# One core, attention over a cached context with a feed-forward beside it: softmax maxima and head blocks moved from TensorE to VectorE, softmax sums taken once at the end, projections in 512 columns

## The chip, the core and the metric

The kernel runs on one core of a Trainium2 chip. The metric is the device time of one execution in microseconds (us), the median of several executions of the same program. Engines are named as the profile names them: PE is TensorE (PEld its weight loads), DVE VectorE, ACT ScalarE, POOL GpSimd, and SP the engine that issues most DMA transfers.

## What is computed

One decoding step for 4 sequences: a layer norm of `x` (4 x 512), then multi-head attention with one query per sequence over a cached context, and beside it a feed-forward layer; both are added to `x`.

```python
xn = _layernorm(x)                                   # (4, 1, 512)
q  = (xn @ wq).reshape(B, 1, 32, 128).transpose(0, 2, 1, 3)
scores = einsum("bhqd,bhkd->bhqk", q, k_cache) * 128 ** -0.5
o  = einsum("bhqk,bhkd->bhqd", softmax(scores), v_cache)
a  = o.transpose(0, 2, 1, 3).reshape(B, 1, 32 * 128) @ wo
f  = silu(xn @ w1) @ w2                              # F = 1792
return x + a + f
```

All data are 32-bit floats. `k_cache` and `v_cache` have shape 4 x 32 x 4096 x 128, 268 MB each; `wq` and `wo` are 8.4 MB each, `w1` and `w2` 3.7 MB each. All of it is read once.

## The kernel before, in words

**Tiles.** The work goes in T = 32 tiles. Tile `i` is one sequence (`b = i % 4`) and a group of G = 4 heads (`h = i // 4 * 4`): 4 x 4096 cached rows, spread as 128 partitions x R = 128 rows x 128 elements (8.4 MB of keys, and as much of values). Partitions 0 to 31 hold head `h`, 32 to 63 head `h + 1`, and so on (PH = 32 partitions a head).

**Buffers and loads.** `load_tile` (L72) issues one transfer on SP's queue. Key tiles have two buffers (`kpool`), value tiles one (`vpool`). In the loop (L328) iteration `i` issues key tile `i + 1` (L330) and value tile `i` (L337), in that order, all on SP, which waits in order: a key load until `sums` of the tile two back has read its buffer, a value load until `values` of the tile before has read the only value buffer. `w1` and `x` lie at first in a key buffer (`scratch`), `wq` in the value buffer; `wo` takes the value buffer at the end and `w2` a key buffer (L352 to L359, `wo` in two pieces, `w2` in four). The last value tile goes into a key buffer (L339).

**Start (L93 to L223).** Constants, layer norm, `xn` transposed; the hidden layer on PE in four strips of columns (L179), SiLU on ACT (L185), 56 small transposing matmuls (L191) into `hT`; the queries in 128 matmuls of 128 columns (L206), regrouped by head (L218) into `q_h`.

**Each tile.** `queries(n)` (L227) copies the queries of a group of four heads over the partitions by four matmuls into a PSUM buffer `q_ps` (two buffers, one per group; a group serves four tiles). `products` (L241) multiplies 32 rows of the key tile by the query on DVE and lets POOL add the two halves of each row; `sums` (L258) reduces each row to its score. `maxima` (L265) reduces a partition's scores on DVE and transposes the 128 maxima on PE (L269). `softmax` (L272) reduces them to one per head on DVE (L275), copies these to all partitions by a matmul (L279) and a scaled copy on ACT (L281), then takes four exponentials on ACT (L285), which also leave each partition's sum in `l`. `values` (L291) does 32 matmuls of 512 columns into one PSUM bank, four groups of 32 output partitions in turn: each row of that bank has a product for each of NR = 4 rows, of which one is wanted. `heads_out` (L305) sums `l` over a head's partitions by a matmul with `same` (L309), copies the bank to SBUF on ACT (L311), and with DVE's reciprocal (L315) and scaled selection matrix `w_t` (L316) adds the wanted blocks into `o_all` by four matmuls of 128 columns (L320).

**Order.** The loop issues `products(i, 0)`, `softmax(i - 1)`, `values(i - 1)`, the rest of the products and sums, `maxima(i)`, `heads_out(i - 1)`, and in every fourth iteration (`i % B == 1`) the queries of the next group. Each engine runs its own stream in order; the framework's scheduler may move an instruction ahead of earlier ones in the program where data and buffers allow it by its own estimate.

**End (L361 to L385).** The last softmax, values and heads; `o_all` copied (L367), transposed by four matmuls (L370) and copied (L375) to `ot`; then `accumulate` (L135) adds each of 32 rows of `wo` and 14 rows of `w2` to `acc` as four matmuls of 128 columns (L138), 184 in all; one copy (L382) and four small output transfers.

Of the kernel before, what the change touches and what calls it, by code (L numbers as in the profile page):

```python
# [8 lines left out]
F32 = mybir.dt.float32  # L9
# [14 lines left out]
def kernel(  # L24
# [29 lines left out]
    FC = F // P  # L54
    PH = P // G
# [27 lines left out]
    FJ = F // 4  # L83
    h_sb = scratch[:, 4 * D : 4 * D + FJ]
# [10 lines left out]
    same = const.tile([P, P], F32, name="same")  # L95
    nc.gpsimd.memset(same, 0.0)
    for g in range(G):
        nc.gpsimd.memset(
            same[g * PH : (g + 1) * PH, :].rearrange("p (a g) -> p a g", g=G)[:, :, g], 1.0
        )  # L100
    one = const.tile([1, 1], F32, name="one")
    nc.gpsimd.memset(one, 1.0)
# [3 lines left out]

    W0 = H - G
    w_t = const.tile([P, NR, W0 + H], F32, name="w_t")
# [15 lines left out]
        o_all.rearrange("h b d -> h (b d)"), w_t[:, 0, :H], p_t.rearrange("p r g -> p (r g)"),  # L124
# [7 lines left out]
        axis=AX, op=ALU.add,  # L132
    )
# [41 lines left out]

    hp = ps_s.tile([P, FJ], F32, name="sm")
    for c in range(DC):
        for j in range(4):
            nc.tensor.matmul(  # L179
                hp[32 * j : 32 * j + B, :], xnT[:, c, :], w1_t[:, c, j * FJ : (j + 1) * FJ],  # L180
                start=(c == 0), stop=(c == DC - 1),
            )
    for j in range(4):
        rows = slice(32 * j, 32 * j + B)
        nc.scalar.activation(h_sb[rows, :], hp[rows, :], AF.Silu)  # L185
    ht_ps = ps_s.tile([P, FC, B], F32, name="sm")
    h_f = h_sb.rearrange("b (m f) -> b f m", f=FC)
    for f in range(FC):
        for j in range(4):
            rows = slice(32 * j, 32 * j + B)  # L190
            nc.tensor.matmul(  # L191
                ht_ps[32 * j : 32 * j + 32, f, :], h_f[rows, f, :], ident[rows, rows],
                start=True, stop=True,
            )
    hT = const.tile([P, FC, B], F32, name="hT")
    nc.vector.tensor_copy(hT, ht_ps)


    HJ = H // 4
    qp = ps_s.tile([P, Dh], F32, name="sm")  # L200
    for hl in range(HJ):
        for c in range(DC):
            for j in range(4):
                h = HJ * j + hl
                a = PH - B - B * hl
                nc.tensor.matmul(  # L206
                    qp[32 * j : 32 * j + 32, :],
                    xpad[:, c, a : a + PH],
                    wq_t[:, c, h * Dh : (h + 1) * Dh],
                    start=(hl == 0 and c == 0),  # L210
                    stop=(hl == HJ - 1 and c == DC - 1),
                )

    q_all = const.tile([P, Dh], F32, name="q_all")
    nc.vector.tensor_copy(q_all, qp)  # L215
    qh_ps = ps_q.tile([P, B, Dh], F32, name="q_ps")
    for b in range(B):
        nc.tensor.matmul(  # L218
            qh_ps[:H, b, :], ident.rearrange("p (h b) -> p b h", b=B)[:, b, :], q_all,
            start=True, stop=True,  # L220
        )
    q_h = const.tile([H, B, Dh], F32, name="q_h")
    nc.vector.tensor_copy(q_h, qh_ps[:H])  # L223

    q_ps, vs, st, ls = {}, {}, {}, {}

    def queries(n):  # L227

        t = ps_q.tile([P, B, Dh], F32, name="q_ps")
        for g in range(G):  # L230
            h = n * G + g
            nc.tensor.matmul(  # L232
                t[g * PH : (g + 1) * PH].rearrange("p b d -> p (b d)"),
                ident[:H, h : h + 1].to_broadcast([H, PH]),
                q_h.rearrange("h b d -> h (b d)"),
# [29 lines left out]
    def maxima(i):  # L265
        m = small.tile([P, 1], F32, name="m")
        nc.vector.tensor_reduce(m, st[i], axis=AX, op=ALU.max)  # L267
        mt = ps_s.tile([1, P], F32, name="sm")
        nc.tensor.transpose(mt, m, ident)  # L269
        return mt  # L270

    def softmax(i, mt):  # L272
        s = st.pop(i)
        gm = small.tile([1, G], F32, name="gm", bufs=1)
        nc.vector.tensor_reduce(  # L275
            gm, mt.rearrange("o (g m) -> o g m", g=G), axis=AX, op=ALU.max
        )
        mb = ps_s.tile([P, G], F32, name="sm")
        nc.tensor.matmul(mb, one.to_broadcast([1, P]), gm, start=True, stop=True)  # L279
        nb = small.tile([P, G], F32, name="nb", bufs=1)  # L280
        nc.scalar.activation(nb, mb, AF.Copy, scale=-scale)  # L281
        l = small.tile([P, 1], F32, name="l_t")
        for g in range(G):
            rows = slice(g * PH, (g + 1) * PH)
            nc.scalar.activation(  # L285
                p_t[rows, :, g], s[rows, :], AF.Exp, bias=nb[rows, g : g + 1], scale=scale,
                accum_out=l[rows, :],
            )
        ls[i] = l

    def values(i):  # L291
        v, o = vs.pop(i), o_ps
        n = R // NR
        for m in range(n):
            j = 32 * (m % 4)
            rows = slice(m * NR, (m + 1) * NR)
            nc.tensor.matmul(  # L297
# [5 lines left out]
            )  # L303

    def heads_out(i):  # L305

        h, b = i // B * G, i % B
        lt = ps_s.tile([P, 1], F32, name="sm")
        nc.tensor.matmul(lt, same, ls.pop(i), start=True, stop=True)  # L309
# [4 lines left out]
        rl = small.tile([P, 1], F32, name="rl", bufs=1)  # L314
        nc.vector.reciprocal(rl, lt)  # L315
        nc.vector.tensor_scalar_mul(  # L316
            w_t[:, :, W0 : W0 + G], pick.rearrange("p (r g) -> p r g", r=NR), rl
        )
        for r in range(NR):
            nc.tensor.matmul(  # L320
                o_all[:, b, :], w_t[:, r, W0 - h : W0 - h + H], o_sb[:, r, :],
# [96 lines left out]
```

## Time and profile before

| | us |
|---|---|
| median of 3 runs | 1310.15 (1309.88 to 1310.94) |
| the profiled execution | 1309.97 |
| its span, first to last instruction | 1307.9 |
| mean granted TensorE clock in it | 0.646 of full speed |

A row of an instruction group reads: line, engine, operation, output and input names, shapes, count, then busy time and mean duration of one in ns, then the idle time of the engine just before and what ended it. A row of the timeline begins with its start and its duration in us; in brackets is the idle time of the engine before it, and what ended that. One 32-bit matmul shows as two matmul records and two weight-load records. A row of a table by stretches has the stretch and its length, then the busy time and count of PE, PEld, DVE, ACT and POOL, then the granted clock, the DMA engines' mean busy share and GB/s. A row of a DMA queue has its packets, MB, and share of 16 engines' span.

### The profile page before, as it was taken

The page shows a single profiled execution, that of the slowest core. Times are in us where ns is not written, and L with a number is a line of the kernel's source. Part 1 is how long each engine was busy: PE and PEld are TensorE (multiplying, and loading weights), DVE is VectorE, ACT ScalarE, POOL GpSimd, SP SyncE. Part 2 cuts the span into 40 slices and gives each one's busy share as a digit, 9 for nine tenths or more (in the row PEclk, how much of TensorE's full clock was granted, in tenths as well). Part 3 has the DMA queues.
Part 4 walks back from the last instruction along what each step waited for, and adds up shares of the span by engine and source line. Part 5 has one row for each costly group of instructions (what it writes and reads, how often), then busy time and mean ns, then how long its engine had stood idle before and what let it go on. Part 6 is the DMA issues. An engine that isn't in the chain of part 4 may idle for free.

```text
span 1307.9 us, 7983 instructions
## 1 busy us (share of the span) xinstructions
PE 397.9 (30%) x3326; PEld 139.1 (11%) x3326; DVE 911.7 (70%) x439; ACT 97.7 (7%) x329; POOL 511.0 (39%) x144
## 2 busy tenths in 40 slices
PE   3412233320333322133332123332043333113337
PEld 1300011100011100011110001110011111001113
DVE  1499666887666787666687666678666678766660
ACT  1010000000000000000000000000000000000000
POOL 0255333444332444332444433344433344433340
PEclk9656666655666656666665666665566665566669
DMA  9999999999999999999999999999999999999997
GB/s 406 440 425 440 427 437 430 435 435 431 438 427 439 429 436 427 435 433 433 434 429 435 429 437 423 439 429 435 429 423 443 422 443 423 443 421 443 425 427 334
DMA packets 10443, 561.51 MB, mean 429 GB/s; under 512 B 1172, under 2 KB 1188, under 8 KB 1448
## 3 DMA queue, kind: packets, MB, share of 16 engines
q1 hardware_dynamic: 10392, 561.01, 99.4%
q8 instruction: 26, 0.43, 0.1%
q14 instruction: 9, 0.07, 0.0%
q10 hardware_dynamic: 16, 0.00, 0.0%
HBM read 561.00 MB, written 0.01 MB: 429 GB/s over the span
## 4 chain that ended last, share of the span: by engine, by line
DMA 66%; PE 17%; DVE 14%; POOL 3%; issue 0%; SPq 0%; POOLq 0%; DVEq 0%
DMA v_t<-in_A_v_cache_dram 34%; DMA k_t<-in_A_k_cache_dram 29%; PE o_ps L297 15%; DVE k_t L247 9%; DVE s L263 4%; DMA k_t<-in_B_w_dram 3%; POOL k_t L251 3%; PE q_ps L232 1%; DVE s L262 0%; PE sm L269 0%; SPq L359 0%; PE acc L138 0%; DVE gm L275 0%; DVE m L267 0%; SPq L87 0%
## 5 line engine op out<-in xcount | busy, mean ns | idle before, releaser
L251 POOL TENSOR_TENSOR k_t<-k_t 128x2048 f32<-128x2048 f32 (+1 forms) x128 | 508.4, 3983 | 749.5 <-DVE k_t L247 749.5
L247 DVE TENSOR_TENSOR k_t<-k_t,q_ps 128x4096 f32<-128x4096 f32 x128 | 562.4, 4414 | 247.8 <-DMA k_t<-in_A_k_cache_dram 247.8
L297 PE MATMUL o_ps<-v_t,p_t 128*16 128x512 f32 x1984 | 283.2, 735 | 628.7 <-DMA v_t<-in_A_v_cache_dram 624.9
L263 DVE TENSOR_REDUCE s<-k_t 128x32 f32<-128x2048 f32 (+1 forms) x128 | 257.7, 2013 | 11.2 <-POOL k_t L251 11.2
L297 PEld LDWEIGHTS o_ps<-v_t,p_t 128*16 128x16 f32 x1984 | 65.4, 113 | 834.6 <-issue 830.8
L311 ACT ACTIVATE o_sb<-o_ps 128x512 f32<-128x512 f32 x32 | 19.1, 597 | 1081.2 <-PE o_ps L297 1081.2
L262 DVE TENSOR_REDUCE s<-k_t 128x16 f32<-128x2048 f32 x32 | 72.8, 2276 | 0.0
L232 PE MATMUL q_ps<-q_h,ident 32*32 32x512 f32 x64 | 14.0, 974 | 183.2 <-DVE k_t L247 182.5
L285 ACT ACTIVATE p_t<-s,nb 32x128 f32<-32x128 f32 x128 | 66.0, 516 | 2.7 <-ACT nb L281 0.2
L275 DVE TENSOR_REDUCE gm<-sm 1x4 f32<-1x128 f32 x32 | 8.9, 278 | 53.7 <-PE sm L269 53.7
L320 PE MATMUL o_all<-o_sb,w_t 128*32 128x128 f32 x256 | 34.0, 276 | 2.4 <-ACT o_sb L311 0.7
L320 PEld LDWEIGHTS o_all<-o_sb,w_t 128*32 128x32 f32 x256 | 25.8, 110 | 5.4 <-ACT o_sb L311 1.6
L285 ACT ACTIVATION_READ_ACCUMULATOR p_t<-s,nb 32x1 f32 x128 | 25.0, 196 | 0.0
L269 PE MATMUL sm<-ident,m 128*1 128x128 f32 x32 | 8.8, 276 | 42.4 <-DVE m L267 41.9
L232 PEld LDWEIGHTS q_ps<-q_h,ident 32*32 32x32 f32 x64 | 1.6, 128 | 185.7 <-DVE k_t L247 184.1
L279 PE MATMUL sm<-gm,one 1*128 1x4 f32 x64 | 12.5, 264 | 11.9 <-DVE gm L275 11.7
L375 DVE COPY ot<-sm 128x128 f32<-128x128 f32 x1 | 0.3, 292 | 19.3 <-PE sm L370 19.3
L215 DVE COPY q_all<-sm 128x128 f32<-128x128 f32 x1 | 0.3, 292 | 17.6 <-PE sm L206 17.6
L206 PE MATMUL sm<-v_t,xpad 128*32 128x128 f32 x256 | 9.8, 327 | 7.9 <-DMA v_t<-in_A_wq_dram 6.0
L281 ACT ACTIVATE nb<-sm 128x4 f32<-128x4 f32 x32 | 5.6, 174 | 84.7 <-PE sm L279 84.7
L297 PE MATMUL o_ps<-k_t,p_t 128*16 128x512 f32 x64 | 9.4, 753 | 6.6 <-DMA k_t<-in_A_v_cache_dram 6.6
L382 DVE COPY s<-acc 128x128 f32<-128x128 f32 x1 | 0.3, 292 | 15.9 <-PE acc L138 15.9
(66 smaller groups left out, 119.0 us busy)
## 6 DMA issues: line engine op xcount, KB each, us to landing
v_t<-in_A_wo_dram SPq DMA_DIRECT2D x2, 4096.0 KB
k_t<-in_B_w_dram SPq DMA_DIRECT2D x1, 3584.0 KB, 11.5
k_t<-in_B_w_dram SPq DMA_DIRECT2D x1, 1792.0 KB, 33.2
k_t<-in_B_w_dram SPq DMA_DIRECT2D x1, 1024.0 KB, 35.9
k_t<-in_A_k_cache_dram SPq DMA_DIRECT2D x32, 48.3
k_t<-in_B_w_dram SPq DMA_DIRECT2D x1, 512.0 KB, 36.7
v_t<-in_A_v_cache_dram SPq DMA_DIRECT2D x31, 29.4
k_t<-in_B_w_dram SPq DMA_DIRECT2D x1, 256.0 KB, 36.9
```

The costliest lines, as they stand in the source:

```text
L206: nc.tensor.matmul(qp[32 * j : 32 * j + 32, :], xpad[:, c, a : a + PH], wq_t[:, c, h * Dh : (h + 1) * Dh], start=(hl == 0 and c == 0), sto ...
L232: nc.tensor.matmul(t[g * PH : (g + 1) * PH].rearrange("p b d -> p (b d)"), ident[:H, h : h + 1].to_broadcast([H, PH]), q_h.rearrange("h b ...
L247: nc.vector.tensor_tensor(k[:, a:z, :], k[:, a:z, :], q[:, None, :].to_broadcast([P, STEP, Dh]), op=ALU.mult)
L251: nc.gpsimd.tensor_tensor(k[:, a:v, :half], k[:, a:v, :half], k[:, a:v, half:], op=ALU.add)
L262: nc.vector.tensor_reduce(s[:, v:z], k[:, v:z, :], axis=AX, op=ALU.add)
L263: nc.vector.tensor_reduce(s[:, a:v], k[:, a:v, :half], axis=AX, op=ALU.add)
L275: nc.vector.tensor_reduce(gm, mt.rearrange("o (g m) -> o g m", g=G), axis=AX, op=ALU.max)
L279: nc.tensor.matmul(mb, one.to_broadcast([1, P]), gm, start=True, stop=True)
L285: nc.scalar.activation(p_t[rows, :, g], s[rows, :], AF.Exp, bias=nb[rows, g : g + 1], scale=scale, accum_out=l[rows, :],)
L297: nc.tensor.matmul(o[j : j + NR * G, :], p_t[:, rows, :].rearrange("p r g -> p (r g)"), v[:, rows, :].rearrange("p r d -> p (r d)"), start ...
L311: nc.scalar.activation(o_sb.rearrange("p r d -> p (r d)"), o_ps, AF.Copy)
L320: nc.tensor.matmul(o_all[:, b, :], w_t[:, r, W0 - h : W0 - h + H], o_sb[:, r, :], start=False, stop=(i == T - 1 and r == NR - 1),)
```

## The change

Per tile: `maxima` stays on DVE. It puts a partition's maximum into column 0 of a zeroed tile of 32 columns, transposes each 32 x 32 block, reduces along the row, scales over 32 columns and transposes back, so that each partition has its head's scaled maximum; the matmuls at L269 and L279, the reduction at L275 and ACT's copy at L281 go. `softmax` leaves its sums in one tile `l_t` for all tiles, and the per-tile matmul (L309), reciprocal and scaling go; the sums are added and inverted once at the end. `heads_out` multiplies the copied bank by a mask `own` and adds the four blocks on DVE, so that one matmul of 128 columns with a fixed selection matrix is left of four.

Order: the first products of a tile are put behind the last instruction of the tile before's `maxima` on DVE (`issue_after(done)`), and the queries of the next group behind the last matmul of `values(i - 1)` in the iterations with `i % B == 2`.

Start and end: the hidden layer is computed in 16 matmuls of up to 512 columns, with the columns of `w1` taken 14 apart, and transposed by four matmuls of 128 columns of a zeroed tile; `wq` in 32 matmuls of 512 columns, with 16 small ones to regroup; `wo` and the first seven rows of `w2` go as 39 matmuls of 512 columns into a bank of their own (`part`, in a `q_ps` buffer), four groups of output partitions in turn, whose copy is added into `acc` by four matmuls; the last seven rows of `w2` are added as before.

```diff
-    h_sb = scratch[:, 4 * D : 4 * D + FJ]
+    h_sb = scratch[:, 4 * D : 4 * D + FT * P]
...
-    same = const.tile([P, P], F32, name="same")
...
+    ones = const.tile([P, 1], F32, name="ones")
+    nc.gpsimd.memset(ones, 1.0)
+    nc.gpsimd.memset(h_sb, 0.0)
...
+    l_t = const.tile([P, B, H // G, G], F32, name="l_t")
+    nc.gpsimd.memset(l_t, 0.0)
+    m_t = const.tile([P, PH], F32, name="m_t")
+    nc.gpsimd.memset(m_t, 0.0)
...
+    nc.vector.tensor_reduce(
+        w_t[:, W0 : W0 + G], pick.rearrange("p (r g) -> p g r", r=NR), axis=AX, op=ALU.add
+    )
+    own = const.tile([P, NR], F32, name="own")
+    nc.vector.tensor_reduce(
+        own, pick.rearrange("p (r g) -> p r g", r=NR), axis=AX, op=ALU.add
     )
...
+    w1_f = w1_t.rearrange("p c (m f) -> p c f m", f=FC)
     for c in range(DC):
         for j in range(4):
             nc.tensor.matmul(
-                hp[32 * j : 32 * j + B, :], xnT[:, c, :], w1_t[:, c, j * FJ : (j + 1) * FJ],
+                hp[32 * j : 32 * j + B, : FN[j] * P],
+                xnT[:, c, :],
+                w1_f[:, c, F0[j] : F0[j] + FN[j], :],
                 start=(c == 0), stop=(c == DC - 1),
             )
...
+    for t in range(FT):
+        nc.tensor.matmul(
+            ht_ps[:, t],
+            h_sb[:, t * P : (t + 1) * P],
+            ident.rearrange("p (j m) -> p j m", j=4)[:, :, :B],
+            start=True, stop=True,
+        )
...
-                    wq_t[:, c, h * Dh : (h + 1) * Dh],
-                    start=(hl == 0 and c == 0),
-                    stop=(hl == HJ - 1 and c == DC - 1),
+                    wq_t[:, c, n * G * Dh : (n + 1) * G * Dh],
+                    start=(m == 0 and c == 0),
+                    stop=(m == NM - 1 and c == DC - 1),
...
     def maxima(i):
-        m = small.tile([P, 1], F32, name="m")
-        nc.vector.tensor_reduce(m, st[i], axis=AX, op=ALU.max)
-        mt = ps_s.tile([1, P], F32, name="sm")
-        nc.tensor.transpose(mt, m, ident)
-        return mt
+        nc.vector.tensor_reduce(m_t[:, :1], st[i], axis=AX, op=ALU.max)
+        mt = small.tile([P, PH], F32, name="mt", bufs=1)
+        nc.vector.transpose(mt, m_t)
+        gm = small.tile([P, 1], F32, name="gm", bufs=1)
+        nc.vector.tensor_reduce(gm, mt, axis=AX, op=ALU.max)
+        mb = small.tile([P, PH], F32, name="mb", bufs=1)
+        nc.vector.tensor_scalar_mul(mb, gm.to_broadcast([P, PH]), -scale)
+        nb = small.tile([P, PH], F32, name="nb", bufs=1)
+        return nb, nc.vector.transpose(nb, mb).ins
 
-    def softmax(i, mt):
+    def softmax(i, nb):
         s = st.pop(i)
...
-        mb = ps_s.tile([P, G], F32, name="sm")
-        nc.tensor.matmul(mb, one.to_broadcast([1, P]), gm, start=True, stop=True)
-        nb = small.tile([P, G], F32, name="nb", bufs=1)
-        nc.scalar.activation(nb, mb, AF.Copy, scale=-scale)
-        l = small.tile([P, 1], F32, name="l_t")
...
-                p_t[rows, :, g], s[rows, :], AF.Exp, bias=nb[rows, g : g + 1], scale=scale,
-                accum_out=l[rows, :],
-            )
-        ls[i] = l
+                p_t[rows, :, g], s[rows, :], AF.Exp, bias=nb[rows, :1], scale=scale,
+                accum_out=l_t[rows, i % B, i // B, g : g + 1],
+            )
...
     def heads_out(i):
-        lt = ps_s.tile([P, 1], F32, name="sm")
-        nc.tensor.matmul(lt, same, ls.pop(i), start=True, stop=True)
...
-        rl = small.tile([P, 1], F32, name="rl", bufs=1)
-        nc.vector.reciprocal(rl, lt)
-        nc.vector.tensor_scalar_mul(
-            w_t[:, :, W0 : W0 + G], pick.rearrange("p (r g) -> p r g", r=NR), rl
-        )
-        for r in range(NR):
-            nc.tensor.matmul(
-                o_all[:, b, :], w_t[:, r, W0 - h : W0 - h + H], o_sb[:, r, :],
-                start=False, stop=(i == T - 1 and r == NR - 1),
-            )
+        nc.vector.tensor_tensor(
+            o_sb, o_sb, own[:, :, None].to_broadcast([P, NR, Dh]), op=ALU.mult
+        )
+        o_1 = small.tile([P, Dh], F32, name="o_1", bufs=1)
+        nc.vector.tensor_reduce(o_1, o_sb.rearrange("p r d -> p d r"), axis=AX, op=ALU.add)
+        nc.tensor.matmul(
+            o_all[:, b, :], w_t[:, W0 - h : W0 - h + H], o_1, start=False, stop=(i == T - 1)
+        )
...
-        products(i, 0)
+        with tc.issue_after(done) if i > 0 else nullcontext():
+            products(i, 0)
         if i > 0:
-            softmax(i - 1, mt)
+            softmax(i - 1, nb)
         if i > 0:
-            values(i - 1)
+            with tc.issue_after(values(i - 1)):
+                if i % B == 2 and i + B < T + 2:
+                    queries(i // B + 1)
...
-        mt = maxima(i)
+        nb, done = maxima(i)
         if i > 0:
             heads_out(i - 1)
-        if i % B == 1 and i + B < T:
-            queries(i // B + 1)
...
+    ls_ps = ps_s.tile([H, B], F32, name="sm")
+    for b in range(B):
+        nc.tensor.matmul(
+            ls_ps[:, b : b + 1], l_t[:, b].rearrange("p n g -> p (n g)"), ones,
+            start=True, stop=True,
+        )
+    rl = const.tile([H, B], F32, name="rl")
+    nc.vector.reciprocal(rl, ls_ps)
     o_row = const.tile([H, B, Dh], F32, name="o_row")
-    nc.scalar.activation(o_row, o_all, AF.Copy)
+    nc.vector.tensor_tensor(
+        o_row, o_all, rl[:, :, None].to_broadcast([H, B, Dh]), op=ALU.mult
+    )
...
-    for c in range(H):
-        accumulate(ot[:, c, :], wo_t[:, c, :])
-    for f in range(FC):
-        accumulate(hT[:, f, :], w2_t[:, f, :], stop=(f == FC - 1))
+    part = ps_q.tile([P, D], F32, name="q_ps")
+    nc.vector.memset(part, 0.0)
+    rows = [(ot[:, c, :], wo_t[:, c, :]) for c in range(H)]
+    rows += [(hT[f], w2_t[:, f, :]) for f in range(W2_CUTS[0])]
+    for c, (a, w) in enumerate(rows):
+        j = 32 * (c % 4)
+        nc.tensor.matmul(
+            part[j : j + B, :], a, w, start=(c < 4), stop=(c >= len(rows) - 4)
+        )
+    part_sb = small.tile([P, NR * Dh], F32, name="o_sb", bufs=1)
+    nc.scalar.activation(part_sb, part, AF.Copy)
+    accumulate(pick[:, :B], part_sb)
+    for f in range(W2_CUTS[0], FC):
+        accumulate(hT[f], w2_t[:, f, :], stop=(f == FC - 1))
```

86 lines of the change are left out of this document (38 added, 48 removed).

## The prediction

> **What bounds the kernel now.** First the page: the engines' busy shares, the DMA queues, the chain that ended last.
>
> ```profile
> PE 397.9 (30%) x3326; PEld 139.1 (11%) x3326; DVE 911.7 (70%) x439; ACT 97.7 (7%) x329; POOL 511.0 (39%) x144
> q1 hardware_dynamic: 10392, 561.01, 99.4%
> q8 instruction: 26, 0.43, 0.1%
> DMA 66%; PE 17%; DVE 14%; POOL 3%; issue 0%; SPq 0%; POOLq 0%; DVEq 0%
> ```
>
> No engine is near its span, but the packets of the data queue fill 99.4% of 16 DMA engines' time. Yet the chain gives PE 17% and DVE 14%. The timeline of one late period tells which is true: SP's issues, the values' start on PE, the next products' start on DVE.
>
> ```profile
> 1188.64 0.33 SPq L76 DMA_DIRECT2D v_t<-in_A_v_cache_dram  x1
> 1189.06 0.38 SPq L76 DMA_DIRECT2D k_t<-in_A_k_cache_dram  x1
> 1197.88 8.75 DVE L247 TENSOR_TENSOR k_t<-k_t,q_ps 128x4096 f32<-128x4096 f32 x2 [8.44 <-DMA k_t<-in_A_k_cache_dram]
> 1217.34 9.37 PE L297 MATMUL o_ps<-v_t,p_t 128*16 128x512 f32 x64 [26.73 <-DMA v_t<-in_A_v_cache_dram]
> 1226.78 0.33 SPq L76 DMA_DIRECT2D v_t<-in_A_v_cache_dram  x1
> 1236.59 8.75 DVE L247 TENSOR_TENSOR k_t<-k_t,q_ps 128x4096 f32<-128x4096 f32 x2 [9.02 <-DMA k_t<-in_A_k_cache_dram]
> ```
>
> The value tile issued at 1188.64 lands near 1217.2, the key tile behind it at 1236.5: one 8.4 MB tile each 19.4 us, one behind the other. PE's 9.37 us do set when the next value load is issued (1226.78), but a key tile is then still in the queue for 9.8 us more. So PE is on the chain of issues and not on that of bytes: the queue has work when the new transfer joins it. All 16 engines together, over the whole middle:
>
> ```profile
> 51.80:1236.60 1184.80, 340.19 (x2361) 107.68 (x2361) 876.08 (x402) 88.75 (x310) 492.54 (x124) 0.63 1.00 433
> 51.80 8.75 DVE L247 TENSOR_TENSOR k_t<-k_t,q_ps 128x4096 f32<-128x4096 f32 x2 [5.25 <-DMA k_t<-in_A_k_cache_dram]
> 148.82 8.75 DVE L247 TENSOR_TENSOR k_t<-k_t,q_ps 128x4096 f32<-128x4096 f32 x2 [9.55 <-DMA k_t<-in_A_k_cache_dram]
> 188.07 8.75 DVE L247 TENSOR_TENSOR k_t<-k_t,q_ps 128x4096 f32<-128x4096 f32 x2 [4.91 <-DMA k_t<-in_A_k_cache_dram]
> ```
>
> The share is 1.00 at 433 GB/s. The key landings show the only loss there: most pairs of tiles take 38.71 us (1197.88 to 1236.59), a few 39.25 (148.82 to 188.07). From 51.80 to 1236.59 there land 31 key and 30 value tiles; at 38.71/2 each that is 1180.7 us, and it took 1184.8: **4.1 us of excess**. What shares the 16 engines is instruction code. PE's 3326 matmul and 3326 weight-load records are 6652 instructions; 0.43 MB over them is 65 bytes each, and 26 packets are 16.5 KB or 256 instructions each. So queue 8 is PE's own program. 0.1% of 16 x 1307.9 us over 26 packets is 0.8 us a packet (0.4 to 1.2 with the rounding), on one engine; a tile has landed when its last engine is done, so the engine hit most often sets the landings. That the excess is these packets is my inference; nothing in the views names it.
>
> **The end**, by the same timeline (value tile 31 lands, then wo in two halves, then w2 in four pieces):
>
> ```profile
> 1275.33 9.39 PE L297 MATMUL o_ps<-k_t,p_t 128*16 128x512 f32 x64 [6.63 <-DMA k_t<-in_A_v_cache_dram]
> 1277.02 0.17 PEld L297 LDWEIGHTS o_ps<-k_t,p_t 128*16 128x16 f32 x4 [0.68 <-issue]
> 1277.87 0.17 PEld L297 LDWEIGHTS o_ps<-k_t,p_t 128*16 128x16 f32 x4 [0.68 <-issue]
> 1282.84 0.11 PEld L297 LDWEIGHTS o_ps<-k_t,p_t 128*16 128x16 f32 x4 [0.32 <-issue]
> 1283.27 0.11 PEld L297 LDWEIGHTS o_ps<-k_t,p_t 128*16 128x16 f32 x4 [0.32 <-issue]
> 1284.80 0.60 ACT L311 ACTIVATE o_sb<-o_ps 128x512 f32<-128x512 f32 x1 [16.54 <-PE o_ps L297]
> 1287.28 1.12 PE L370 MATMUL sm<-o_row,up 32*128 32x128 f32 x8 [0.77 <-ACT o_row L367]
> 1288.44 0.29 DVE L375 COPY ot<-sm 128x128 f32<-128x128 f32 x1 [19.27 <-PE sm L370]
> 1288.79 3.68 PE L138 MATMUL acc<-v_t,ot 128*4 128x128 f32 x128 [0.38 <-DVE ot L375]
> 1294.77 3.68 PE L138 MATMUL acc<-v_t,ot 128*4 128x128 f32 x128 [2.31 <-DMA v_t<-in_A_wo_dram]
> 1299.08 1.06 PE L138 MATMUL acc<-k_t,hT 128*4 128x128 f32 x32 [0.63 <-DMA k_t<-in_B_w_dram]
> 1302.21 1.06 PE L138 MATMUL acc<-k_t,hT 128*4 128x128 f32 x32 [0.20 <-DMA k_t<-in_B_w_dram]
> 1303.49 1.05 PE L138 MATMUL acc<-k_t,hT 128*4 128x128 f32 x24 [0.23 <-DMA k_t<-in_B_w_dram]
> 1304.68 0.29 DVE L382 COPY s<-acc 128x128 f32<-128x128 f32 x1 [15.94 <-PE acc L138]
> ```
>
> PE waits for data at 1294.77, 1299.08, 1302.21 and 1303.49. Only the matmuls behind the very last piece, the copy at 1304.68 and the output lie behind the bytes, and the change leaves these as they are.
>
> **The change, part by part.** *Per tile.* The groups by line and shape give what goes and the prices of what comes:
>
> ```profile
> L320 PE MATMUL o_all<-o_sb,w_t 128*32 128x128 f32 x256 | 34.0, 276 | 2.4 <-ACT o_sb L311 0.7
> L279 PE MATMUL sm<-gm,one 1*128 1x4 f32 x64 | 12.5, 264 | 11.9 <-DVE gm L275 11.7
> L309 PE MATMUL sm<-l_t,same 128*128 128x1 f32 x64 | 9.2, 213 | 1.4 <-ACT p_t L285 1.4
> L267 DVE TENSOR_REDUCE m<-s 128x1 f32<-128x128 f32 x32 | 9.2, 286 | 1.1
> L151 DVE TENSOR_TENSOR k_t<-k_t 4x512 f32<-4x512 f32 x1 | 0.7, 680 | 0.0
> L179 PE MATMUL sm<-k_t,xnT 128*4 128x448 f32 x32 | 4.5, 724 | 0.3 <-DVE xnT L171 0.3
> ```
>
> PE loses 11 of its 77 records a tile (one at L269, two each at L279 and L309, six of eight at L320). DVE gains a multiply and a reduction over 512 elements (0.68 us each) and, in the maxima, two transposes, a reduction and a scaling of 32 columns for two small operations and a reduction that go. Neither that reduction nor a transpose is in the trace; for the first I take L151's time, which has as many elements, for a transpose between nothing and that 0.68 I take L267's 0.29, the nearest by shape. Net some 1.4 + 0.6 = 2 us, at most 3.5. Cover: DVE idles 8 to 10 us for each key tile (the brackets above), and key loads are queued a whole value tile early (1189.06, behind a value load that itself finds the queue full). Price at the end: 0. The new order, first products behind the maxima, costs up to 1.2 us of the same idle time; softmax then starts at once and has 19 us until its value tile lands. If that cover were gone, DVE would have to be late by 8 us.
>
> *Queries behind the values.* In some periods PE now waits for a query buffer with the values queued behind it:
>
> ```profile
> 948.23 1.93 PE L232 MATMUL q_ps<-q_h,ident 32*32 32x512 f32 x8 [30.44 <-DVE k_t L247]
> 960.04 0.33 SPq L76 DMA_DIRECT2D v_t<-in_A_v_cache_dram  x1
> 964.65 8.75 DVE L247 TENSOR_TENSOR k_t<-k_t,q_ps 128x4096 f32<-128x4096 f32 x2 [3.83 <-DMA k_t<-in_A_k_cache_dram]
> ```
>
> The value load is then issued 4.6 us before the key tile in flight lands, not 9.8: late, but not too late. The new place gives the 5 us back; behind the values the buffer is two blocks old, so PE waits for nothing. Price: 0.
>
> *Start.* wq becomes 32 matmuls of 512 columns, as many as one tile's values (9.4 us by the row at 1275.33), and the hidden layer 16 with columns taken 14 apart, which no row shows; between nothing and four times L179's 4.5 us the start's work ends some us earlier to 14 later. Key tile 0 lands at 51.8 whatever they do, and DVE's own work (876 us over 32 tiles, 27 each) then sets the next key load, with a value tile still in the queue. Price: 0.
>
> *End.* From 1284.7: copy 0.6, multiply and reduction 1.4, the head matmul and the sums 0.8, reciprocal and multiply 0.8, transposition 1.1, copy 0.3, some 0.5 of handing over: `ot` at 1290.2 instead of 1288.7. Two matmuls of 512 columns take 0.43 us at full clock (1282.84 to 1283.27), so a half of wo takes 3.4: 1293.6, before 1294.7. The second half ends at 1298.2, before 1299.0; seven rows of w2 take 1.5 to 1300.6. Then PE waits for ScalarE's copy of `part` (0.7) with the last w2 rows queued behind: four small matmuls more, 1301.8, and the next rows come at 1302.1. Slack 1.1, 0.8 and 0.3 us. Price 0, at most +0.5.
>
> *Code.* Matmul records: 352 fewer in the tiles, 192 at L206, 104 at L191, 226 in the projections; 24 more at L218, 8 for the sums: 842 of 3326, **25%**, or 6 to 7 packets of queue 8. A quarter of the 4.1 us of excess is 1.0 us. Bounds: 0, if the same engine is hit as often, and 2.2, if it loses most of its hits.
>
> **Sum:** -1.0 from the profiled execution's 1309.97 us (span 1307.9 and 2.1 around it) is 1309.0; that execution lay 0.2 below the median of the runs, so **1309.2**.
>
> **Rivals.** *Faster: the code packets cost more than their share.* If the whole excess goes with them, -4.1: 1306.1. For: they are all that shares the engines. Against: three quarters of them stay.
>
> *Slower, at the end: the clock.* The windows after tile 30's values:
>
> ```profile
> 1263.10:1266.50 3.40, 3.09 (x31) 1.48 (x20) 2.13 (x6) 1.12 (x4) 0.00 (x0) 1.00 0.80 347
> 1266.50:1269.90 3.40, 0.82 (x6) 0.46 (x4) 0.40 (x2) 1.71 (x8) 0.00 (x0) 0.99 1.25 540
> 1269.90:1273.30 3.40, 0.00 (x0) 0.00 (x0) 0.00 (x0) 0.00 (x0) 0.00 (x0) 0.50 0.83 352
> ```
>
> After 3.4 us with 0.82 of PE work the clock fell to a half. In the new chain 1284.7 to 1288.1 holds about 0.8. At half clock a pair of matmuls takes 0.85 (1277.02 to 1277.87); if that lasted to the end, wo would end at 1290.2 + 13.8, seven rows 3.0 later, the copy 0.8, and 32 small matmuls 3.7: 1311.5 for 1304.6, **+6.9**, 1317. Against it: at 1275.33 the clock was back within 5.5 us of work, and wo is 14 us of it; back by 1296, the slack takes it up. It decides if the half clock lasts past about 1297. The Trainium skill, "TensorE: Matmul & The Clock Gate", "HAM oscillation", warns of just this, PE gaps over about 3.4 us that throttle the clock again; by that rule the change would lose, and the rows agree on the drop.
>
> *Slower, in the middle.* If the heads' multiply and reduction stood on DVE behind a whole tile's products, their matmul would hold the next values on PE until some 30 us after a key landing; 9.4 later the value load is issued at 39.5 to 40, after the queue ran dry at 38.7: about 1 us in each of 30 tiles, 1339. It begins where the heads end 28.7 us after a landing; I see no reason for that order.
>
> *It doesn't do what it says* (queries still early): same time, 1309.
>
> **Chances.** Forecast 0.84; packets worth more 0.07; clock 0.04; dry queue 0.03; not done 0.02. A measurement of this kernel tells about 0.2%, 2.6 us, from no change: faster 0.07, same 0.86, slower 0.07. The range, 1307.2 to 1311.4, takes in the code's bound of 2.2, 0.5 of the end and a short dip of the clock.
>
> **What would show it.** Right: queue 1 near 99.4%, 433 GB/s in the middle, 19 or 20 packets on queue 8, key landings 38.7 us apart, no DVE wait at L232, `acc` waiting for w2. Wrong: a DMA share under 0.98 in the middle, a last value load issued behind a key landing, or `acc` at half clock after 1297.

## The result, and the profile after

The changed kernel takes **1308.18 us** (median of 22 runs, 1307.80 to 1309.80) against 1310.11 (22 runs beside them, 1309.71 to 1311.00): ratio **0.9986** (95% interval 0.9980 to 0.9992), or 1.9 us less. That is no change by the 0.2% of the prediction, though the interval excludes 1. Its profiled execution took 1307.80, with a span of 1306.0.

The page of the kernel after: busy time and instructions of the engines, the queues, the chain that ended last.

```profile
PE 354.7 (27%) x2484; PEld 87.0 (7%) x2484; DVE 973.8 (75%) x540; ACT 92.6 (7%) x297; POOL 510.9 (39%) x142
...
q1 hardware_dynamic: 10392, 561.01, 99.4%
q8 instruction: 19, 0.31, 0.1%
q14 instruction: 10, 0.08, 0.0%
...
DMA 70%; PE 22%; another core or an unknown queue 4%; DVE 2%; issue 2%; POOL 0%; ACT 0%; SPq 0%; POOLq 0%; ACTq 0%
```

PE has 842 matmul records fewer (2484 for 3326) and 43 us less work; DVE has 62 us more. Queue 8 brings 19 code packets instead of 26, and the data queue fills 99.4% as before. PE's share of the chain has grown, from 17% to 22%, while PE does less: the chain of issues still says nothing of the bytes.

The middle, from the first key tile's landing to the last one's: the whole stretch, then rows of the timeline.

```profile
51.90:1235.40 1183.50, 297.65 (x2042) 70.72 (x2042) 933.20 (x495) 83.84 (x279) 492.72 (x124) 0.61 1.00 433
```

```profile
905.33 8.47 PE L310 MATMUL o_ps<-v_t,p_t 128*16 128x512 f32 x64 [26.63 <-DMA v_t<-in_A_v_cache_dram]
913.73 1.06 PE L250 MATMUL q_ps<-q_h,ident 32*32 32x512 f32 x8
...
1196.71 8.75 DVE L265 TENSOR_TENSOR k_t<-k_t,q_ps 128x4096 f32<-128x4096 f32 x2 [8.26 <-DMA k_t<-in_A_k_cache_dram]
...
1235.41 8.75 DVE L265 TENSOR_TENSOR k_t<-k_t,q_ps 128x4096 f32<-128x4096 f32 x2 [7.92 <-DMA k_t<-in_A_k_cache_dram]
```

1183.50 us instead of 1184.80, at the same share of 1.00 and the same 433 GB/s: 1.3 us of the gain is here. The period is 38.70 us as before (1196.71 to 1235.41), and DVE still waits 6 to 9 us for each key tile with 1.84 us more work in it ((933.20 - 876.08) / 31). The queries at L250 follow the values at once, with no wait in brackets. Taking 61 tiles at 38.71/2 from the stretch, as the prediction did, leaves an excess of 2.8 us, which was 4.1.

The end of the same kernel, by the timeline:

```profile
1274.14 8.39 PE L310 MATMUL o_ps<-k_t,p_t 128*16 128x512 f32 x64 [6.50 <-DMA k_t<-in_A_v_cache_dram]
...
1282.65 0.60 ACT L323 ACTIVATE o_sb<-o_ps 128x512 f32<-128x512 f32 x1 [15.42 <-issue]
...
1284.01 1.02 DVE L330 TENSOR_REDUCE o<-o_sb 128x128 f32<-128x512 f32 x1
...
1287.73 0.29 DVE L396 COPY ot<-sm 128x128 f32<-128x128 f32 x1 [1.53 <-PE sm L391]
...
1288.08 9.93 PE L404 MATMUL q_ps<-v_t,ot 128*4 128x512 f32 x64 [0.38 <-DVE ot L396]
...
1300.55 0.40 PE L148 MATMUL acc<-o_sb,pick 128*4 128x128 f32 x8 [0.76 <-ACT o_sb L408]
...
1302.31 0.11 PEld L148 LDWEIGHTS acc<-k_t,ht_sb 128*4 128x4 f32 x8 [0.31 <-DMA k_t<-in_B_w_dram]
1302.78 0.29 DVE L414 COPY s<-acc 128x128 f32<-128x128 f32 x1 [14.76 <-PE acc L148]
```

From value tile 31 (1274.14) to the last copy are 28.64 us; before, 1275.33 to 1304.68, 29.35: another 0.7. PE's last act is still a wait for the last piece of `w2` (0.31 at 1302.31). So the end is still set by bytes, and these came sooner after the value tile.

**What is to be explained**, then: 1.3 us in the middle and 0.7 at the end in two profiled executions, in a queue that was full before and is full after. My theory: code packets of PE, seven fewer, in the middle and the end alike. Rivals: the later queries (a value load that joins the queue earlier), PE's busy time as such, and the shape of the end.

### The profile page after: what moved, and what is told of

It reads as the page before. It is cut to its first block, busy times and chain, and to the rows that moved or that the text cites. A ratio compares the mean times of both kernels' runs of the same rounds, so it can differ in the third digit from the quotient of the medians.

```text
span 1306.0 us, 6301 instructions
## 1 busy us (share of the span) xinstructions
PE 354.7 (27%) x2484; PEld 87.0 (7%) x2484; DVE 973.8 (75%) x540; ACT 92.6 (7%) x297; POOL 510.9 (39%) x142
## 3 DMA queue, kind: packets, MB, share of 16 engines
q1 hardware_dynamic: 10392, 561.01, 99.4%
## 4 chain that ended last, share of the span: by engine, by line
DMA 70%; PE 22%; another core or an unknown queue 4%; DVE 2%; issue 2%; POOL 0%; ACT 0%; SPq 0%; POOLq 0%; ACTq 0%
DMA v_t<-in_A_v_cache_dram 61%; PE o_ps L310 20%; DMA k_t<-in_A_k_cache_dram 4%; DMA k_t<-in_A_v_cache_dram 3%; DMA v_t<-in_A_wq_dram 2%; DVE k_t L265 1%; PE q_ps L404 1%; PE sm L219 1%; DVE s L281 1%; POOL k_t L269 0%; DVE s L280 0%; PE acc L148 0%; PE sm L391 0%; PE q_ps L233 0%
## 5 line engine op out<-in xcount | busy, mean ns | idle before, releaser
L269 POOL TENSOR_TENSOR k_t<-k_t 128x2048 f32<-128x2048 f32 (+1 forms) x128 | 508.6, 3985 | 748.5 <-DVE k_t L265 748.5
L281 DVE TENSOR_REDUCE s<-k_t 128x32 f32<-128x2048 f32 (+1 forms) x128 | 257.7, 2014 | 11.9 <-POOL k_t L269 11.9
L326 DVE TENSOR_TENSOR o_sb<-o_sb,own 128x512 f32<-128x512 f32 x32 | 21.7, 678 | 26.5 <-ACT o_sb L323 26.4
L331 PE MATMUL o_all<-o,w_t 128*32 128x128 f32 x64 | 15.7, 336 | 88.7 <-DVE o L330 88.7
L330 DVE TENSOR_REDUCE o<-o_sb 128x128 f32<-128x512 f32 x32 | 32.8, 1024 | 3.2
L331 PEld LDWEIGHTS o_all<-o,w_t 128*32 128x32 f32 x64 | 4.9, 118 | 118.0 <-DVE o L330 118.0
L404 PE MATMUL q_ps<-v_t,ot 128*4 128x512 f32 x64 | 9.9, 788 | 0.4 <-DVE ot L396 0.4
L285 DVE TENSOR_REDUCE m_t<-s 128x1 f32<-128x128 f32 x32 | 9.1, 285 | 1.1
L293 DVE STREAM_TRANSPOSE nb<-mb 128x32 f32<-128x32 f32 x32 | 6.8, 212 | 3.3
L219 PE MATMUL sm<-v_t,xpad 128*32 128x512 f32 x64 | 8.5, 690 | 1.3 <-DMA v_t<-in_A_wq_dram 1.3
L250 PE MATMUL q_ps<-q_h,ident 32*32 32x512 f32 x64 | 8.5, 599 | 0.8 <-DVE q_h L240 0.8
```

Source lines behind the costliest of these rows:

```text
L219: nc.tensor.matmul(qp[32 * j : 32 * j + 32, :], xpad[:, c, a : a + PH], wq_t[:, c, n * G * Dh : (n + 1) * G * Dh], start=(m == 0 and c == ...
L269: nc.gpsimd.tensor_tensor(k[:, a:v, :half], k[:, a:v, :half], k[:, a:v, half:], op=ALU.add)
L281: nc.vector.tensor_reduce(s[:, a:v], k[:, a:v, :half], axis=AX, op=ALU.add)
L326: nc.vector.tensor_tensor(o_sb, o_sb, own[:, :, None].to_broadcast([P, NR, Dh]), op=ALU.mult)
L330: nc.vector.tensor_reduce(o_1, o_sb.rearrange("p r d -> p d r"), axis=AX, op=ALU.add)
L331: nc.tensor.matmul(o_all[:, b, :], w_t[:, W0 - h : W0 - h + H], o_1, start=False, stop=(i == T - 1))
```

## The experiments

Each time is a median over its runs; the kernel before lay at 1310.10 to 1310.19 beside them.

**q_only**: the kernel before, with only its queries moved behind the values.

```diff
-            values(i - 1)
+            with tc.issue_after(values(i - 1)):
+                if i % B == 2 and i + B < T + 2:
+                    queries(i // B + 1)
...
-        if i % B == 1 and i + B < T:
-            queries(i // B + 1)
```

> The kernel before with one part of the change alone: the queries of the next group behind the values; as many PE instructions as before (6652). Three theories. Code: PE's own program, loaded in packets by the same DMA engines, delays the engine it hits, so the time goes with the count of PE instructions and not with their work: no change here, 1310.1. Early loads: the value loads that the early queries delay by 5 us in seven tiles cost the time: the whole gain, 1308.2, and in the trace the key landings move closer. End: the projections at the end, in fewer matmuls, give it: no change, 1310.1.

Measured: 1310.09 us (11 runs, 1309.74 to 1310.57), ratio 1.0000 (0.9991 to 1.0008), with 26 packets on queue 8. The move is worth nothing, as priced, within an interval of some 1 us either way. That rival falls.

**end_only**: the kernel before, with only the end in 512 columns.

```diff
-    for c in range(H):
-        accumulate(ot[:, c, :], wo_t[:, c, :])
-    for f in range(FC):
+    part = ps_q.tile([P, D], F32, name="q_ps")
...
+    rows = [(ot[:, c, :], wo_t[:, c, :]) for c in range(H)]
+    rows += [(hT[:, f, :], w2_t[:, f, :]) for f in range(W2_CUTS[0])]
...
+    accumulate(pick[:, :B], part_sb)
+    for f in range(W2_CUTS[0], FC):
```

> The kernel before with the end of the change alone: wo and the first seven rows of w2 in 39 matmuls of 512 columns into a bank of their own, the copy, and four matmuls to add it. 452 PE instructions fewer, nearly 2 of 26 code packets. Code: a quarter of the gain, -0.3 to -0.7, 1309.4 to 1309.8. End: at least the 0.7 us by which the stretch from the last value tile's landing to the end is shorter after the change, 1309.4, or the whole gain, 1308.2. Early loads: 1310.1.

Measured: 1309.33 us (11 runs, 1308.84 to 1310.29), ratio 0.9995 (0.9986 to 1.0003): 0.8 less by the medians, with 24 packets. Seven of the 11 runs lie below the fastest of the 22 of before shown above. Most likely a gain, but its interval holds 1, and two packets went with it: by itself it doesn't tell shape from code.

**pad13**: the changed kernel, with 13 matmuls of one column behind the values of each of 31 tiles. They put the PE records back (3290 for 3326 of before), but only 22 us of work.

```diff
+    def pad(n):
+        t = ps_s.tile([P, 1], F32, name="sm")
+        for _ in range(n):
+            nc.tensor.matmul(t[:B, :], ident[:, :B], ones, start=True, stop=True)
...
                     queries(i // B + 1)
+                pad(13)
```

> The changed kernel with 13 matmuls of one column and four weights in each of 31 tiles, behind the values, in a PSUM tile that nobody reads; they bring the PE instructions back to the number before (some 1600 more, 6.3 packets of code) and take PE about half a microsecond a tile in which it is idle for 25. Code: +1.1 to +1.9, 1309.3 to 1310.1. Early loads and End: no change, 1308.2.

Measured: **1309.23 us** (11 runs, 1308.98 to 1310.26), ratio 0.9994 (0.9985 to 1.0002): 1.05 slower than the changed kernel, a little under the expected range. Its fastest run is slower than 20 of the 22 of the changed kernel. The page has the code back:

```profile
q8 instruction: 26, 0.43, 0.1%
```

In its profiled execution the middle is 1184.11 us (0.6 more than after), and, with the changed kernel's own end, value tile 31 to last copy is 29.49 us (0.85 more). The landing of the last piece of `w2` shows why. First pad13's timeline, then the DMA issues, KB and us from issue to landing, of pad13 and of the kernel after:

```profile
1274.53 9.42 PE L310 MATMUL o_ps<-k_t,p_t 128*16 128x512 f32 x64 [7.16 <-DMA k_t<-in_A_v_cache_dram]
...
1303.55 0.11 PEld L148 LDWEIGHTS acc<-k_t,ht_sb 128*4 128x4 f32 x8 [0.31 <-DMA k_t<-in_B_w_dram]
```

```profile
k_t<-in_B_w_dram SPq DMA_DIRECT2D x1, 256.0 KB, 37.1
```

```profile
k_t<-in_B_w_dram SPq DMA_DIRECT2D x1, 256.0 KB, 35.0
```

The end's instructions are the same in both; the piece came later. Of the 2.1 us, 0.9 are an earlier issue in pad13 and 0.4 the value tile's own later landing; 0.85 are left behind value tile 31 (1303.55 less 1274.53, against 1302.31 less 1274.14). So tiny matmuls placed in the tiles took back the end's gain as well as half of the middle's.

**pad104**: the same with 104 in place of 13.

```diff
-                pad(13)
+                pad(104)
```

> The changed kernel with 104 such matmuls in each of 31 tiles: 12896 PE instructions more, 50 packets of code, some 4 to 6 us of PE's idle time a tile. Code: between 0.18 us a packet (2.8 us of excess over 16 packets in the middle after the change) and 0.28 (1.9 us less for 7 packets fewer): +9 to +14, 1317 to 1322, the queue of instruction packets at 69 or 70, and key landings irregularly more than 38.7 us apart. Early loads and End: no change, 1308.2.

Measured: **1317.70 us** (5 runs, 1317.22 to 1318.40), ratio 1.0058 (1.0044 to 1.0071): 9.5 more than after, for 51 packets more, 0.19 us each. The page's rows of PE and queue 8, then key landings by the timeline:

```profile
PE 518.3 (39%) x8932; PEld 253.6 (19%) x8932; DVE 974.3 (74%) x540; ACT 92.7 (7%) x297; POOL 510.8 (39%) x142
...
q8 instruction: 70, 1.15, 0.3%
```

```profile
149.21 8.75 DVE L265 TENSOR_TENSOR k_t<-k_t,q_ps 128x4096 f32<-128x4096 f32 x2 [6.42 <-DMA k_t<-in_A_k_cache_dram]
...
187.90 8.75 DVE L265 TENSOR_TENSOR k_t<-k_t,q_ps 128x4096 f32<-128x4096 f32 x2 [6.72 <-DMA k_t<-in_A_k_cache_dram]
...
228.16 8.75 DVE L265 TENSOR_TENSOR k_t<-k_t,q_ps 128x4096 f32<-128x4096 f32 x2 [8.76 <-DMA k_t<-in_A_k_cache_dram]
...
266.86 8.75 DVE L265 TENSOR_TENSOR k_t<-k_t,q_ps 128x4096 f32<-128x4096 f32 x2 [6.94 <-DMA k_t<-in_A_k_cache_dram]
...
305.57 8.75 DVE L265 TENSOR_TENSOR k_t<-k_t,q_ps 128x4096 f32<-128x4096 f32 x2 [7.53 <-DMA k_t<-in_A_k_cache_dram]
```

The cost is not spread: intervals of 38.69, 40.26, 38.70 and 38.71. Eight jumps of some 1.55 in the middle make nearly all of the excess, and in the other intervals PE's packets cost nothing. DVE waits 6 to 10 us for every key tile all the while: no engine is late, the landing is.

The trace also records when each packet starts, and that tells more than the views above. The eight long intervals hold the 9th, 17th, 25th and so on to the 65th packet of queue 8, and no other interval holds one of these. So every eighth packet of PE's code costs some 1.55 us here and the seven between cost nothing, 0.19 each in the mean. The kernel before shows the same round of eight in smaller parts: its intervals are 39.25, 39.36, 38.80 and 39.02 at the 5th, 9th, 11th and 12th packet and 39.25, 39.37, 38.80 and 39.00 at the 13th, 17th, 19th and 20th, 1.6 over 38.71 in each round. That fits packets taken to the DMA engines in turn, of which only those cost that fall on the engine which finishes the tile; the records don't name the engine.

**work6**: the other half of the question, PE's work without its instructions: six matmuls of 512 columns behind each tile's values in place of the 13.

```diff
+        t = ps_s.tile([P, 512], F32, name="sm")
...
+                t.rearrange("p (a m) -> p a m", a=4)[:B], ident[:, :B],
+                ident[:, None, :].to_broadcast([P, 4, P]), start=True, stop=True,
...
+                pad(6)
```

> The changed kernel with 6 matmuls of 512 columns in each of 31 tiles, behind the values, into a tile that nobody reads: about as much more PE time a tile (some 5 us) as the 104 small matmuls took, but 744 instructions, 2.9 code packets. Code: 0.19 us a packet, as the run with 104 small ones gave (9.5 us for 51 packets), so +0.5, 1308.7. If it was PE's busy time, or what PE reads and writes, that slowed the transfers: +9, 1317.

The added groups, of work6 and then of pad104 (count, busy time and mean ns of one, idle time before):

```profile
L338 PE MATMUL sm<-ident 128*4 128x512 f32 x372 | 164.7, 592 | 0.0
```

```profile
L338 PE MATMUL sm<-ones,ident 128*4 128x1 f32 x6448 | 168.3, 163 | 51.0 <-issue 51.0
```

Measured: **1308.21 us** (11 runs, 1307.96 to 1309.07), ratio 0.9985 (0.9976 to 0.9994): 0.03 from the changed kernel. Some 165 us of PE time cost 9.5 us as 6448 records and nothing as 372. The rival of busy time falls. The 0.5 that I gave its three packets (22) did not appear either: its two longest intervals, 40.25 and 39.99, hold the 9th and the 17th packet, and its 22 stop short of a 25th.

Over all twelve profiled executions, 73 single intervals between key landings hold no packet of queue 8 or 14 at all. None of them is longer than 38.73 us, so every longer one has a code packet in it.

**pad_act** and **pad_act20**: is it PE's code or any code? 80, then 20, copies of one column on ScalarE behind each tile's softmax.

```diff
...
+    junk = const.tile([P, 1], F32, name="junk")
+
+    def pad(n):
+        for _ in range(n):
+            nc.scalar.activation(junk, ones, AF.Copy)
...
-            softmax(i - 1, nb)
+            with tc.issue_after(softmax(i - 1, nb)):
+                pad(80)
```

> The changed kernel with 80 copies of one column on ScalarE in each of 31 tiles, behind the exponentials, some 15 us of time in which ScalarE is idle: 2480 more instructions for ScalarE, none for PE. If any engine's program is loaded by the same DMA engines: 0.16 MB more in the instruction queues, and at 0.19 us for each 16.5 KB +1.8, 1310.0. If only PE's code costs: no change, 1308.2.

> The changed kernel with 20 copies of one column on ScalarE in each of 31 tiles, a quarter of the earlier run's: 620 instructions, 4.8 packets of 8 KB. In the run with 80 most landings came 0.68 us late, as if each of its 19 packets hit one and the same DMA engine; the time rose by 11.1 us and not 19 x 0.68 = 12.9, so that engine would have had some 1.8 us in hand. One engine: 4.8 x 0.68 - 1.8 = +1.5, 1309.7. Spread over engines in turn, with a price of 0.58 a packet: +2.8, 1311.0. Contention by ScalarE's work, a quarter of 11.1: +2.8, 1311.0.

pad_act measured **1319.27 us** (5 runs, 1318.59 to 1319.49), ratio 1.0067 (1.0054 to 1.0079): 11.1 more than after, against 1.8 expected. A miss by a factor of six. Its queue rows, the middle as one stretch, and key landings by the timeline:

```profile
q8 instruction: 19, 0.31, 0.1%
q14 instruction: 29, 0.24, 0.0%
```

```profile
51.90:1246.50 1194.60, 296.96 (x2042) 70.72 (x2042) 933.75 (x495) 575.34 (x2715) 492.79 (x124) 0.61 1.00 431
```

```profile
383.61 8.75 DVE L265 TENSOR_TENSOR k_t<-k_t,q_ps 128x4096 f32<-128x4096 f32 x2 [6.85 <-DMA k_t<-in_A_k_cache_dram]
...
422.99 8.75 DVE L265 TENSOR_TENSOR k_t<-k_t,q_ps 128x4096 f32<-128x4096 f32 x2 [7.78 <-DMA k_t<-in_A_k_cache_dram]
...
461.69 8.75 DVE L265 TENSOR_TENSOR k_t<-k_t,q_ps 128x4096 f32<-128x4096 f32 x2 [7.90 <-DMA k_t<-in_A_k_cache_dram]
...
501.08 8.75 DVE L265 TENSOR_TENSOR k_t<-k_t,q_ps 128x4096 f32<-128x4096 f32 x2 [7.58 <-DMA k_t<-in_A_k_cache_dram]
```

ScalarE's code comes on queue 14, in packets of 8 KB (0.24 MB over 29). The transfers stay queued without a gap (share 1.00, DVE waiting 6 to 9 us), yet 20 of 28 intervals take 39.36 to 39.71, most of them 39.38 or 39.39, and not 38.70. It is the code and not ScalarE's work: the 80 copies are in every tile, but by the packet records all 20 long intervals hold a packet of queue 14, and of the eight short ones only one does. 19 packets at 0.58 us are half as large as PE's and three times as dear: as if nearly every one fell on the engine that ends last. pad_act20 was to test that: 1308.87 us (11 runs, 1308.03 to 1309.65), ratio 0.9987 (0.9978 to 0.9996), 0.7 more than after for four packets (14), in place of 1.5 by one reading and 2.8 by the others. The sign and the kind of jump are there (five intervals of 39.38 to 39.40, each with a packet of queue 14 in it), the size is half of the nearest reading: seven other intervals hold such a packet too and are not longer than 38.85.

**pad_dve40**: the same with 40 copies on VectorE behind each tile's maxima.

```diff
+            nc.vector.tensor_copy(junk, ones)
...
+        if i > 0:
+            with tc.issue_after(done):
+                pad(40)
```

> The changed kernel with 40 copies of one column on VectorE in each of 31 tiles, behind the maxima, where it is idle for 7 us: 1240 instructions, 9.7 packets of 8 KB. If VectorE's program is loaded as ScalarE's is, all by one DMA engine: 9.7 x 0.68 = 6.6 less what that engine has in hand (0 to 1.8), +4.8 to +6.6, 1313 to 1314.8. If its packets go to engines in turn: +1 to +2, 1309.2 to 1310.2. If VectorE's code costs nothing: 1308.2, as long as the 4 us of work stay inside its idle time.

Measured: 1317.10 us (5 runs, 1316.97 to 1317.75), ratio 1.0052 (1.0040 to 1.0065): 8.9 more than after, for nine packets, on queue 14 too (19), near 1 us each. It isn't a clean price, since the copies ate DVE's cover, by the timeline and by the middle in two stretches:

```profile
452.70 7.44 DVE L339 COPY junk<-ones 128x1 f32<-128x1 f32 x40
...
500.13 8.75 DVE L265 TENSOR_TENSOR k_t<-k_t,q_ps 128x4096 f32<-128x4096 f32 x2 [0.19 <-DMA k_t<-in_A_k_cache_dram]
```

```profile
52.17:447.96 395.79, 94.80 (x646) 22.64 (x650) 376.28 (x525) 27.34 (x90) 174.70 (x44) 0.61 1.00 433
447.96:1244.76 796.80, 203.58 (x1404) 48.84 (x1396) 734.93 (x1171) 55.92 (x189) 318.33 (x81) 0.62 1.00 430
```

7.4 us a tile leave DVE 0.2 to 1.6 us of idle time ahead of a key tile, and from the first one until 500.13 it never waits for one. The DMA share stays 1.00 throughout, which speaks against a dry queue. Behind 500.13 the packet records separate code from copies: the copies are in every tile, but of 19 intervals nine of the 11 with a packet of queue 14 take 39.65 to 39.81, and of the eight without one seven take 38.65 to 38.74 and one 39.11. How much of the 8.9 was lost ahead of 500.13, and to what, stays open.

**end_small**: the changed kernel, with the end of before (184 matmuls of 128 columns).

```diff
-    part = ps_q.tile([P, D], F32, name="q_ps")
...
-    accumulate(pick[:, :B], part_sb)
-    for f in range(W2_CUTS[0], FC):
+    for c in range(H):
+        accumulate(ot[:, c, :], wo_t[:, c, :])
+    for f in range(FC):
```

> The changed kernel with the end of the kernel before: the projections in matmuls of 128 columns into one bank, 452 PE instructions more. By the run with the end alone it should cost what that gained, +0.8, 1309.0, whatever the cause; the code theory at the mean price of a packet gives +0.3, 1308.5.

Measured: 1308.81 us (11 runs, 1308.18 to 1311.98), ratio 0.9994 (0.9985 to 1.0003): 0.6 more than after by the medians, with a spread of 3.8 us that settles little. The timeline of its end:

```profile
1301.13 2.15 PE L148 MATMUL acc<-k_t,ht_sb 128*4 128x128 f32 x71 [1.80 <-issue]
...
1303.34 0.29 DVE L404 COPY s<-acc 128x128 f32<-128x128 f32 x1 [15.10 <-PE acc L148]
```

Here PE doesn't wait for `w2` at the last but idles 1.80 us with nothing that the profile names, in a burst of small matmuls. The kernel before has such a gap too, of 1.03, and then waits for `w2` all the same. The packet records show what PE waits for: a packet of queue 8 ends at 1299.69 in end_small and at 1299.73 in the kernel before, and PE goes on 1.44 us later in both (1301.13 and 1301.17). In pad104 PE has 19 such gaps among its pads, 51.0 us in all, and each ends 1.2 to 1.6 us behind a packet of queue 8. So a burst of small matmuls can outrun its own code. In end_small the last copy then starts 1.51 us behind the last packet of `w2`, in the kernel after 1.00: that is 0.5 of the 0.6.

**pad_tail**: 150 matmuls of one column between the values of tiles 30 and 31, to price code at the end alone.

```diff
+            done_v = values(i - 1)
...
+    with tc.issue_after(done_v):
+        pad(150)
     softmax(T - 1, nb)
```

> The changed kernel with 150 matmuls of one column at the end of the last loop iteration, between the values of tile 30 and those of tile 31, where PE is idle for 6 us: 600 instructions, 2.3 code packets, all loaded in the last 45 us. If what the end gained (0.8 us when it was changed alone, with 2 packets fewer) was code alone: +0.8 to +0.9, 1309.0 to 1309.1; at the mean price of 0.19 us a packet +0.4, 1308.6. If it was the shape of the end's work: no change, 1308.2.

Measured: 1309.16 us (11 runs, 1308.12 to 1310.45), ratio 0.9992 (0.9983 to 1.0001), 1.0 more than after. It doesn't answer the question: the pads outlasted PE's idle time, with a wait of 3.41 us among them that is another of these gaps.

```profile
1274.31 1.24 PE L338 MATMUL sm<-ones,ident 128*4 128x1 f32 x44 [3.41 <-issue]
...
1276.39 8.10 PE L310 MATMUL o_ps<-k_t,p_t 128*16 128x512 f32 x61
```

The last values begin late with no wait for data in brackets, and everything behind them is PE's own lateness; the last `w2` rows no longer wait for their data.

## Why the prediction was right, and where not

The sum was right in sign and mechanism: 1309.2 forecast, 1308.2 measured, inside the range and inside "no change". By its steps:

- **What bounds the kernel** held: share 1.00 and 433 GB/s in the middle, a period of 38.70, DVE idle 6 to 9 us a tile, `acc` waiting for `w2` at the last.
- **Per tile**: DVE's extra was put at 2 us, at most 3.5, and is 1.84. The terms inside were off both ways: a transpose takes 0.21 for the 0.29 taken, the reduction over four strided blocks 1.02 for 0.68 taken from a contiguous one. All of it is covered, as said.
- **Queries**: price 0, and q_only gives 1310.09. An earlier place among SP's issues did not become an earlier landing, since the transfer joined a queue that had work.
- **Start**: price 0; the first key tile is used at 51.91 instead of 51.80.
- **Code**: 25% of the records and seven packets (6 to 7 forecast) were to be worth 1.0 us of the 4.1 of excess; the middle of the profiled executions gained 1.3, and putting the records back cost 1.05 in all (pad13). The inference that nothing in the views named is now shown: records cost (pad104), the same PE time without records does not (work6), and no interval without a code packet is long. A packet was taken at 0.8 us (0.4 to 1.2); in the kernel after the median of their durations on record is 1.07. What the sum had as a share of the packets is in truth a cost by steps, one for every eight.
- **End**: this is the term that was mis-sized. It was priced at 0, at most +0.5, with the chain's slacks; it came out 0.7 better in the profile. The slacks were right (`ot` copied 5.1 us after the bank's copy begins, 5.2 forecast), but the bytes behind which they lay moved. I had put the code term on the middle alone and held the landings of the end fixed. In pad13 the last `w2` piece lands 0.85 us later behind value tile 31 with the very same end, so these landings pay for packets too. The packet records point to one packet: from the last key tile's use to the end of the last packet of `w2` it takes 66.3 to 66.4 us in eight of the twelve executions, the kernel after among them, and 67.1 to 67.6 in the three whose 25th packet of queue 8 falls there (before, q_only, pad13). The kernel after has only 19. end_only, with 24, takes 66.8, which this does not explain.
- **The faster rival** (all of the excess goes) fell: 2.8 of 4.1 us stay with 19 of 26 packets, nearly in proportion.
- **The clock rival** happened in part. The windows of the end of the kernel after:

```profile
1282.60:1286.00 3.40, 0.41 (x2) 0.14 (x2) 2.19 (x3) 0.60 (x1) 0.00 (x0) 1.00 1.05 453
1286.00:1289.40 3.40, 2.67 (x16) 1.34 (x20) 0.50 (x2) 0.00 (x0) 0.00 (x0) 0.66 0.99 426
1289.40:1292.80 3.40, 3.40 (x20) 0.59 (x16) 0.00 (x0) 0.00 (x0) 0.00 (x0) 0.50 0.90 384
1292.80:1296.20 3.40, 3.40 (x32) 0.71 (x28) 0.00 (x0) 0.00 (x0) 0.00 (x0) 0.83 0.98 411
1296.20:1299.60 3.40, 3.40 (x34) 0.53 (x26) 0.00 (x0) 0.00 (x0) 0.00 (x0) 1.00 0.72 289
```

After a stretch with 0.41 of 3.4 us busy the clock falls to 0.50, and is full again by 1296.2, ahead of the 1297 from which it would have decided. The first rows of `wo` ran at half clock and cost nothing: PE's next weight loads still waited for the first piece of `w2`, at 1297.90.

**The account.** 1.9 us less: 1.05 comes back with the code by the medians of pad13, 1.4 by its landings, and the queries are worth 0 (q_only). The landings, by the packet records: from the first key tile's use to the end of the last packet of `w2` it takes 1249.8 to 1250.0 us with 19 to 22 packets (after, end_small, work6, pad_tail), 1251.1 with 24 (end_only), 1251.3 to 1251.9 with 26 (pad13, q_only, before) and 1259.2 with 70 (pad104): steps, and not a price for each packet. The end's new shape gives nothing beside that, since the last copy starts 1.01 us behind the last packet of `w2` in the kernel before, 1.04 in end_only and 1.00 in the kernel after.

The 0.6 us by which the kernel before lands behind pad13, with 26 packets each, is mostly something else. The intervals between key landings without a jump take 38.72 us in the mean in the three kernels with the old tiles (before, q_only, end_only) and 38.70 to 38.71 in the nine with the new ones; 0.017 from the kernel before to pad13, over 30.6 tiles, is 0.5 us. What in the tiles does it is open; pad13, which has PE's records back, keeps the shorter interval. Open too is why end_only's 24 packets cost part of a step.

## What to carry to other kernels

When the DMA engines are full, an instruction is also traffic: count the instructions as packets on the data engines before calling an edit free on an idle engine, and count them for the small transfers that end the kernel too. Expect the cost in steps: a few packets more can cost nothing, and the next one a whole step. To tell an engine's time from its instructions, add the same busy time once in many small instructions and once in few large ones. An engine's share of the chain that ended last can rise while it does less; where the DMA share is 1.00, read the landings and not the chain.

## What the runs showed of the hardware that was not expected

Code of different engines has different prices here: 0.19 us a packet of 16 KB in the mean for PE (51 more in pad104, in jumps of 1.55 at every eighth packet), 0.58 us a packet of 8 KB for ScalarE (19 more in pad_act, in jumps of 0.68 at nearly every one), and close to 1 us for VectorE with its cover gone (nine more in pad_dve40, in jumps of 0.96). That the packets of queue 14 stay on one DMA engine and PE's go round is the reading that fits the jumps; no record here names a packet's engine, and pad_act20's 0.17 us a packet does not fit a fixed price. The Trainium skill, "Runtime: NRT & Kernel Launch", "Instruction fetch mechanics", says that code is refilled by DMA in blocks of 16 KiB, 256 instructions, at a cost "mostly hidden". The size agrees for PE (16,384 bytes a packet by the records) and not for queue 14 (8,192); and where the transfers fill every DMA engine, the cost was measured, not hidden, for the data and for PE's own bursts alike.

The full clock came back some 6 us into PE's unbroken work: that began at 1288.08, and a mean of 0.83 in the stretch from 1292.80 puts the rise near 1294.0 (1.16 us at 0.50, the rest of 3.4 at 1). The prediction had 5.5 at most, from the kernel before.
